# Attention loaded and computed by pairs of heads, the first batch's norm split into three steps, and leftover rows on a second DMA queue

## The chip, the cores and the metric

The kernel runs on one core of a Trainium2 chip. The metric is device time in microseconds (us); lower is better. The kernel before takes 851.52 us, the median of 9 runs (851.2 to 853.03).

Engines: PE (TensorE) multiplies matrices, DVE (VectorE) and ACT (ScalarE) work elementwise, SP (SyncE) issues DMAs. ACT can issue DMAs too. PE writes to PSUM banks, which DVE and ACT read.

## The reference, cut to what matters

```python
kv  = np.einsum('bhsd,bhse->bhde', k, v)        # 8 batches, 8 heads, 576 rows, 64 columns
out = np.einsum('bhsd,bhde->bhse', q, kv)
rms = np.sqrt(np.mean(out * out, axis=-1, keepdims=True) + 1e-06)
attn = out / rms * g_norm
x = attn.transpose(0, 2, 1, 3).reshape(8 * 576, 8 * 64)
a, b = x @ w1, x @ w2                           # 512 -> 1024
result = ((a * b) @ w3) @ w_out                 # 1024 -> 1024 -> 512
```

q, k, v and the result are fp32. The four weight matrices arrive as 64-bit floats and are converted on the chip.

## The kernel before, in words

The 576 rows of a batch are split into 512 rows (`G`), which are handled as a group of their own, and 64 leftover rows. The leftover rows of two batches make one tile of 128 rows, and those of all eight batches make a ninth group. The kernel computes `w3 @ w_out` once (the "fold") and then needs two products per group: the gates (`x @ w1`, `x @ w2`, multiplied) and the projection.

**The stages.** First comes the head: load batch 0, compute its attention. Then come the gates of group 0, made by plain matmuls in `gate` (L379), eight blocks `f` of 128 columns; block `f` needs its piece of w1 and w2, converted by `convert`. Then the fold: for each of eight blocks of w3, `turn_w3` (transposes, L406) and `fold_block` (L419), with the attention of batch 1 in pieces between them. Then project group 0, and a loop over groups `T` = 1 to 8: gates by a Strassen-Winograd scheme (`winograd`, L432) with the attention of batch `T + 1` in eight pieces between its products, then the projection, by `winograd` too.

**The attention of a batch** has these steps, and each works on half of the heads, four at a time:
- `load_half` (L91, L99): k, v and q of four heads, 512 KB each, and the leftover rows of k and v (`kl`, `vl`, 64 KB each). `load_left` (L105) loads the leftover rows of q (`ql`) for all heads.
- `kv` (L232): k transposed times v, 64 columns by 64, two heads above each other, five row blocks with the leftover rows as the last one. The result goes into the block-diagonal `kv_bd` by two DVE copies (L247) and two ACT copies (L245).
- `q_t` (L254): four transposes of q, then an ACT copy to `qT` (L256). It is called twice for each half.
- `product` (L295): q times kv, then `norm`: square on ACT (L272), sum on DVE (L274), square root on ACT (L280), reciprocal and multiply on DVE (L281, L282).
- `turn` (L327): four transposes, then ACT scales by `g_norm` into `xT` (L331).
- for odd batches `q_t_left` (L264), `product_left` (L312) and `turn_left` (L336) do the same for the leftover rows of two batches.

**Order.** PE's order is written out by hand over the whole kernel. In the head and the gates of group 0 the orders of DVE, ACT and SP are written out by hand as well; afterwards a scheduler orders these three. Every DMA goes out on SP's queue, in order. PSUM has five banks `mm` and three banks `at`; attention uses `at`. `keep_warm` (L215) issues matmuls whose result nobody reads.

In the head, batch 0 runs by halves: `kv0`, `q_t` twice, `product` twice, then the second half with the turns between. All of a product's norm is issued with it.

**Weights.** `load_raw` (L128) loads 1 MB of 64-bit words into one of four buffers; ACT (L142, L143) and DVE (L144, L147, L150, L154) convert it. `convert_next` converts the next block of a fixed list and then issues the load of the block four places on, which waits for that buffer. So SP's queue in the gate stage is a row of raw loads, with the loads of batch 1 between them; `load_left(1)` is the last thing that this stage issues, behind the raw loads.

**Pieces.** From batch 1 on, `attention(b)` returns eight lists of steps, and the fold or the gates call one list at each of eight places. In the fold a piece stands between `turn_w3` and `fold_block`. Before, the leftover rows have their places in the last three pieces:

```python
if b % 2:
    pieces[5] += [(q_t_left,)]
    pieces[6] += [(product_left,)]
    pieces[7] += [(turn_left,)]
```

Of the kernel before, what the change touches and what calls it, by code (L numbers as in the profile page):

```python
# [19 lines left out]
def kernel(  # L20
# [29 lines left out]
    nc = tc.nc  # L50
# [16 lines left out]
    inp = ctx.enter_context(tc.tile_pool(name="inp", bufs=1))  # L67
# [6 lines left out]
    early = tc.tile_pool(name="early", bufs=1)  # L74
# [6 lines left out]
    q_left = {}  # L81

    HB = H // 2

    def load_half(b, half, pool):

        heads = slice(half * HB, (half + 1) * HB)
        tiles = []
        for name, src in (("k", k), ("v", v), ("q", q)):
            t = pool.tile([P, HB, J * D], FP32, name=f"{name}_sb")  # L90
            nc.sync.dma_start(  # L91
                out=t, in_=src[b, heads, 0:G, :].rearrange("h (p j) d -> p h (j d)", j=J)
            )
            tiles.append(t)
            if name == "q":
                continue
            left = pool.tile([L, HB, D], FP32, name=f"{name}l_sb")
            tiles.append(left)
            nc.sync.dma_start(out=left, in_=src[b, heads, G:S, :].rearrange("h p d -> p h d"))  # L99
        loaded[b, half] = tiles  # L100

    def load_left(b):
        if b % 2 == 0:
            q_left[b // 2] = inp.tile([P, H, D], FP32, name="ql_sb")
        nc.sync.dma_start(  # L105
            out=q_left[b // 2][(b % 2) * L:(b % 2 + 1) * L],
            in_=q[b, :, G:S, :].rearrange("h p d -> p h d"),
        )
# [25 lines left out]
    def convert(dst, raw):  # L134
        if raw.dtype == FP32:
            nc.vector.tensor_copy(out=dst, in_=raw)
            return
        words = raw.bitcast(U32).rearrange("p (n w) -> p n w", w=2)
        lo, hi = words[:, :, 0], words[:, :, 1]
        low = conv_pool.tile([P, 1024], FP32, name="low", bufs=2)  # L140
        dst_bits, low_bits = dst.bitcast(U32), low.bitcast(U32)
        nc.scalar.activation(low, lo, AF.Copy, scale=2.0 ** -51, bias=2.0)  # L142
        nc.scalar.activation(dst, hi.bitcast(FP32), AF.Abs)  # L143
        nc.vector.tensor_scalar(  # L144
            out=dst, in0=dst, scalar1=LEAST, scalar2=MOST, op0=ALU.max, op1=ALU.min
        )
        nc.vector.tensor_scalar(  # L147
            out=dst_bits, in0=dst_bits, scalar1=3, scalar2=None, op0=ALU.logical_shift_left
        )
        nc.vector.scalar_tensor_tensor(  # L150
            out=low_bits, in0=hi, scalar=0x80000000, in1=low_bits,
            op0=ALU.bitwise_and, op1=ALU.bitwise_or,
        )
        nc.vector.tensor_tensor(out=dst_bits, in0=dst_bits, in1=low_bits, op=ALU.add)  # L154
# [27 lines left out]
    def convert_next(what):  # L182
# [9 lines left out]
        convert(dst, raws[n])  # L192
        converted.append(n)
        load_next()

# [5 lines left out]
    nc.scalar.activation(const.tile([P, 1], FP32, name="warm"), eps_col, AF.Sqrt)  # L201
# [16 lines left out]
    def attention(b):  # L218
# [4 lines left out]
        def kv(half):  # L223
            k_sb, kl_sb, v_sb, vl_sb, _ = loaded[b, half]
            n = HB // 2
            kv_ps = bank(ps_at, "at")[:, 0:n * D].rearrange("p (r e) -> p r e", r=n)
            for r in range(n):
                for j in range(J + 1):
                    cols = slice(j * D, (j + 1) * D)
                    for e in range(2):  # L230
                        h = 2 * r + e
                        nc.tensor.matmul(  # L232
                            kv_ps[e * D:(e + 1) * D, r, :],
                            lhsT=k_sb[:, h, cols] if j < J else kl_sb[:, h, :],
                            rhs=v_sb[:, h, cols] if j < J else vl_sb[:, h, :],
                            start=(j == 0),
                            stop=(j == J),
                        )
            for i in range(2):
                rows = slice(i * D, (i + 1) * D)  # L240
                to = bd[rows, half * HB:(half + 1) * HB, rows]
                to = to.rearrange("p (r e) d -> p r e d", e=2)
                for e in range(2):
                    if i:
                        nc.scalar.copy(to[:, :, e, :], kv_ps[e * D:(e + 1) * D])  # L245
                    else:
                        nc.vector.tensor_copy(out=to[:, :, e, :], in_=kv_ps[e * D:(e + 1) * D])  # L247

        def q_t(i, half):

            q_sb = loaded[b, half][-1]
            qt_ps = bank(ps_at, "at").rearrange("p (h t) -> p h t", h=HB)
            for h in range(HB):
                nc.tensor.transpose(qt_ps[:, h, :], q_sb[:, h, i * P:(i + 1) * P], ident)  # L254
            qT[i, half] = work.tile([P, HB, P], FP32, name="qT", bufs=4)
            nc.scalar.copy(qT[i, half], qt_ps)  # L256
# [10 lines left out]
        def norm(o_ps, dst):  # L267
# [11 lines left out]
            )  # L279
            nc.scalar.activation(inv, inv, AF.Sqrt, scale=1.0 / D, bias=eps_col)  # L280
            nc.vector.reciprocal(inv, inv)  # L281
# [9 lines left out]
        def product(i, half):  # L291

            o_ps = bank(ps_at, "at")
            for h in range(HB):
                nc.tensor.matmul(  # L295
                    o_ps[:, h * P:(h + 1) * P],
                    lhsT=qT[i, half][:, h, :],
                    rhs=bd[:, half * HB + h, :],
                    start=True,
                    stop=True,  # L300
                )
            st[i, half] = work.tile([P, 2, HB, D], FP32, name="xn", bufs=3)
            norm(o_ps, st[i, half].rearrange("p j h d -> p h j d"))

        def product_left():
            xn = st["left"] = work.tile([P, H, D], FP32, name="xn", bufs=3)
            for e in range(2):
# [11 lines left out]
                norm(o_ps, xn.rearrange("p (r e) d -> p r e d", e=2)[:, :, e:e + 1, :])  # L319

        def turn(i, half):

            n = HB // 2
            t_ps = bank(ps_at, "at").rearrange("p (r j t) -> p r j t", r=n, j=2)
            for j in range(2):
                for r in range(n):
                    nc.tensor.transpose(  # L327
                        t_ps[:, r, j, :], st[i, half][:, j, 2 * r:2 * r + 2, :], ident
                    )
            dst = x[:, half, i].rearrange("p r (j t) -> p r j t", j=2)  # L330
            nc.scalar.activation(dst, t_ps, AF.Copy, scale=g_col)  # L331
# [10 lines left out]

        if b == 0:

            return {name: lambda f=f, a=a: f(*a) for name, f, a in (
                (f"{f.__name__}{''.join(map(str, a))}", f, a)
                for f, *a in [(kv, 0), (kv, 1)] + [
                    (f, i, half) for f in (q_t, product, turn) for i in range(2) for half in range(2)
                ]
            )}  # L350

        pieces = []
        for half in range(2):
            pieces += [
                [(kv, half), (q_t, 0, half)],
                [(product, 0, half), (q_t, 1, half)],
                [(product, 1, half), (turn, 0, half)],
                [(turn, 1, half)],
            ]
        if b % 2:  # L360
            pieces[5] += [(q_t_left,)]
            pieces[6] += [(product_left,)]
            pieces[7] += [(turn_left,)]
# [230 lines left out]
    with tc.manual_schedule(  # L594
# [3 lines left out]
        load_half(0, 0, inp)  # L598
        load_half(0, 1, early_pool)
        g_src = g_norm.rearrange("(d o) -> d o", o=1)  # L600
        for e in range(2):
            nc.sync.dma_start(out=g_col[e * D:(e + 1) * D, :], in_=g_src)
        for _ in range(RAW):
            load_next()
        load_left(0)
        first = attention(0)
        keep_warm(16)
        for name in ("kv0", "q_t00", "q_t10", "product00", "product10"):
            first[name]()
        keep_warm(4)  # L610
        for name in ("kv1", "q_t01", "q_t11", "turn00", "product01", "turn10", "product11"):
            first[name]()
        keep_warm(4)
        for name in ("turn01", "turn11"):
            first[name]()
# [3 lines left out]
        for _ in range(2):  # L619
            convert_next("w")  # L620
        for f in range(KF):
            convert_next("w" if f + 2 < KF else "w3")
            if f % 2:
                convert_next("w_out")
            gate(0, f)
            if f == 3:
                load_half(1, 0, inp)
        load_left(1)
# [4 lines left out]
    for n, i in enumerate(FOLD_ORDER):  # L633
        if n + 2 < KF:
            convert_next("w3")
# [3 lines left out]
        if n == 1:  # L639
            load_half(1, 1, inp)  # L640
        fold_block(i)
    load_half(2, 0, inp)
    load_left(2)
# [11 lines left out]
    for T in range(1, NG):  # L655
        pieces = iter(attention(T + 1) if T + 1 < B else [])

        def between(n=[0]):
            n[0] += 1
            next(pieces, lambda: None)()  # L660
            if T + 1 < B and n[0] == 2:
                load_half(T + 1, 1, inp)
# [4 lines left out]
        if T + 2 < B:  # L667
            load_half(T + 2, 0, inp)
            load_left(T + 2)
# [33 lines left out]
```

## Time and profile before

| what | before |
|---|---|
| median of 9 runs (lowest, highest) | 851.52 us (851.2, 853.03) |
| the profiled execution's own time | 851.31 us |
| span of the profiled execution | 849.2 us |
| mean granted clock of TensorE | 0.993 of full speed |
| PE weight loads busy | 683.4 us (80%) |
| DMA traffic | 59.41 MB, mean 70 GB/s |

The profile shows one execution. The span is the time from its first to its last instruction; the execution's own time is 2.1 us longer. A line such as `L432` is a line of the kernel; `out<-in` names the tiles. Idle time of an engine that does not set the end costs nothing.

By stage, from the chain of work that ended last: head to 32.5 us, gates of group 0 to 89.3, fold to 165, and from there the projection of group 0 and the loop over the groups, to 849.2.

### The profile page before, as it was taken

How to read it: one execution, taken by the hardware profiler on the slowest of the kernel's cores; microseconds unless marked ns; L12 is line 12 of the kernel's file. 1: busy time of each engine (PE TensorE's matmuls, PEld its weight loads, DVE VectorE, ACT ScalarE, POOL GpSimd, SP SyncE). 2: the span in 40 equal slices, each digit the busy share in tenths (PEclk: the TensorE clock that was granted, in tenths of full speed). 3: DMA queues.
4: the chain of work that ended last, by engine and by line, in shares of the span. 5: the costliest groups of instructions: out<-in, count | busy, mean ns of one | idle time of the engine just before them, and what ended most of it. 6: DMA issues, size and time to landing. Idle time of an engine off the chain costs nothing.

```text
span 849.2 us, 10819 instructions
## 1 busy us (share of the span) xinstructions
PE 830.6 (98%) x4480; PEld 683.4 (80%) x4480; DVE 378.4 (45%) x718; ACT 249.1 (29%) x447; POOL 0.7 (0%) x6
## 2 busy tenths in 40 slices
PE   8599999999999999999999999999999999999997
PEld 7244556588888888888888888888888888888886
DVE  3798963493450455035504550355045503333430
ACT  3645532113321333133213331332133312212220
POOL 0000000000000000000000000000000000000000
PEclk9799999999999999999999999999999999999999
DMA  9768803003201221031012210320120000001002
GB/s 271 228 220 321 280 6 93 1 32 99 57 25 49 81 63 32 34 96 57 25 50 81 63 31 37 94 57 25 50 81 1 2 39 12 1 0 50 1 1 49
DMA packets 52112, 59.41 MB, mean 70 GB/s; under 512 B 14688, under 2 KB 47456, under 8 KB 51040
## 3 DMA queue, kind: packets, MB, share of 16 engines
q1 hardware_dynamic: 52064, 58.73, 22.0%
q8 instruction: 35, 0.57, 0.3%
q14 instruction: 13, 0.11, 0.0%
HBM read 49.28 MB, written 9.44 MB: 69 GB/s over the span
## 4 chain that ended last, share of the span: by engine, by line
PE 96%; DVE 1%; ACT 1%; DMA 1%; issue 0%; SPq 0%; ACTq 0%; DVEq 0%
PE mm L432 71%; PE mm L379 7%; PE mm L419 6%; PE at L295 3%; PE at L232 3%; PE at L254 2%; PE at L327 2%; PE at L312 1%; PE mm L406 1%; DMA v_sb<-in_v_dram 1%; DVE inv L274 0%; DVE xn L282 0%; PE at L336 0%; PE at L264 0%; ACT sq L272 0%
## 5 line engine op out<-in xcount | busy, mean ns | idle before, releaser
L432 PE MATMUL mm<-xT,w_sb 128*128 128x256 f32 x672 | 154.2, 379 | 0.0
L432 PEld LDWEIGHTS mm<-xT,w_sb 128*128 128x128 f32 x672 | 127.7, 190 | 17.4
L432 PE MATMUL mm<-xc,ws 128*128 128x256 f32 x512 | 115.7, 379 | 0.0
L432 PEld LDWEIGHTS mm<-xc,ws 128*128 128x128 f32 x512 | 97.3, 190 | 13.2
L445 ACT COPY u<-mm 128x512 f32<-128x512 f32 x82 | 48.1, 586 | 193.9 <-PE mm L432 193.9
L432 PE MATMUL mm<-w3o_sb,ab 128*128 128x256 f32 x432 | 96.2, 379 | 0.0
L432 PEld LDWEIGHTS mm<-w3o_sb,ab 128*128 128x128 f32 x432 | 82.1, 190 | 11.6 <-issue 0.5
L445 ACT COPY p<-mm 128x512 f32<-128x512 f32 x82 | 48.1, 586 | 139.2 <-PE mm L432 139.2
L432 PE MATMUL mm<-os,as 128*128 128x256 f32 x288 | 63.6, 379 | 0.0
L379 PE MATMUL mm<-xT,w_sb 128*128 128x512 f32 x128 | 56.7, 606 | 6.6 <-DVE w_sb L154 6.6
L432 PEld LDWEIGHTS mm<-os,as 128*128 128x128 f32 x288 | 54.7, 190 | 7.4
L432 PE MATMUL mm<-xc,w_sb 128*128 128x256 f32 x256 | 60.5, 379 | 0.0
L419 PE MATMUL mm<-wo_sb,w3T 128*128 128x512 f32 x128 | 56.4, 593 | 0.0
L274 DVE TENSOR_REDUCE inv<-sq 128x8 f32<-128x512 f32 (+1 forms) x40 | 25.1, 628 | 69.5 <-ACT sq L272 69.5
L379 PEld LDWEIGHTS mm<-xT,w_sb 128*128 128x128 f32 x128 | 24.9, 195 | 38.1 <-issue 30.5
L545 DVE TENSOR_TENSOR c<-mm,u 128x512 f32<-128x512 f32 x32 | 22.0, 688 | 73.9 <-PE mm L432 73.9
L432 PE MATMUL mm<-xT,ws 128*128 128x256 f32 x224 | 53.3, 381 | 0.0
L247 DVE COPY kv_bd<-at 64x128 f32<-64x128 f32 x32 | 9.2, 287 | 95.9 <-PE at L232 95.6
L432 PEld LDWEIGHTS mm<-xc,w_sb 128*128 128x128 f32 x256 | 46.8, 190 | 5.4
L419 PEld LDWEIGHTS mm<-wo_sb,w3T 128*128 128x128 f32 x128 | 23.7, 190 | 26.9 <-issue 26.8
L578 DVE TENSOR_TENSOR o_sb<-mm,u 128x512 f32<-128x512 f32 x9 | 6.2, 692 | 86.4 <-issue 74.0
L432 PEld LDWEIGHTS mm<-xT,ws 128*128 128x128 f32 x224 | 40.7, 190 | 4.7
(87 smaller groups left out, 920.6 us busy)
## 6 DMA issues: line engine op xcount, KB each, us to landing
k_sb<-in_k_dram SPq DMA_DIRECT2D x16, 512.0 KB, 4.4
v_sb<-in_v_dram SPq DMA_DIRECT2D x16, 512.0 KB, 5.3
q_sb<-in_q_dram SPq DMA_DIRECT2D x16, 512.0 KB, 4.0
raw<-in_moe_w_dram SPq DMA_DIRECT2D x16, 512.0 KB, 7.0
raw<-in_moe_w_dram SPq DMA_DIRECT2D x8, 1024.0 KB, 6.2
out_dram<-o_sb SPq DMA_DIRECT2D x16, 512.0 KB, 2.6
raw<-in_moe_w_out_dram SPq DMA_DIRECT2D x4, 1024.0 KB, 5.0
kl_sb<-in_k_dram SPq DMA_DIRECT2D x16, 64.0 KB, 4.3
```

The costliest lines, as they stand in the source:

```text
L232: nc.tensor.matmul(kv_ps[e * D:(e + 1) * D, r, :], lhsT=k_sb[:, h, cols] if j < J else kl_sb[:, h, :], rhs=v_sb[:, h, cols] if j < J else ...
L247: nc.vector.tensor_copy(out=to[:, :, e, :], in_=kv_ps[e * D:(e + 1) * D])
L254: nc.tensor.transpose(qt_ps[:, h, :], q_sb[:, h, i * P:(i + 1) * P], ident)
L274: nc.vector.tensor_reduce(out=inv, in_=sq[:, cols].rearrange("p (h d) -> p h d", d=D), axis=AX.X, op=ALU.add,)
L295: nc.tensor.matmul(o_ps[:, h * P:(h + 1) * P], lhsT=qT[i, half][:, h, :], rhs=bd[:, half * HB + h, :], start=True, stop=True,)
L312: nc.tensor.matmul(o_ps[l * L:(l + 1) * L, r * D:(r + 1) * D], lhsT=st["qT"][rows, r, l * L:(l + 1) * L], rhs=kv_bd[l][rows, 2 * r + e, rows],
L327: nc.tensor.transpose(t_ps[:, r, j, :], st[i, half][:, j, 2 * r:2 * r + 2, :], ident)
L379: nc.tensor.matmul(g_ps, lhsT=w_sb[:, f, w, c, :], rhs=xT[T][:, c // 2, :, c % 2, :], start=(c == 0), stop=(c == NP - 1),)
L419: nc.tensor.matmul(f_ps, lhsT=t[:, j, :], rhs=wo_sb[:, j, :], start=(j == 0), stop=(j == KF - 1))
L432: nc.tensor.matmul(ps[:, u, :], lhsT=lhsT(a_name, u, c), rhs=rhs(b_name, c),  start=(u == 0 and c == 0 and to is None), stop=(c == chunks ...
L445: nc.scalar.copy(t, ps)
L545: nc.vector.tensor_add(c, one, two)
```

## The change: pairs, a split norm, a second queue

- `load_half` becomes `load_pair`: k, v and q of two heads, 256 KB each, in two sets of buffers. The leftover rows of k and v are loaded for all eight heads at once (`load_kv_left`, 128 KB each); for batch 0 from ACT's queue, as is `g_col`.
- `kv`, `q_t`, `product` and `turn` take a pair of heads. Each is called four times per batch. One `q_t` or `product` of a pair has the four transposes or matmuls that one call had before; a `kv` has half as many as before, and its copies are 64 columns wide instead of 128.
- `norm` becomes a generator with two `yield`s: after the sum, and after the square root. Batch 0 uses them to place the parts between the steps of the next pair. All other callers run it through.
- The first block of weights of batch 0's gates is converted in two halves of 512 columns, around the last multiply and turn.
- The pieces of batches 1 to 7 are laid out anew, and the loads are issued from within them. `q_t_left` moves from piece 5 to piece 0.
- The load of `ql` for an even batch is issued in the piece 7 of the batch ahead of it, that for an odd batch in piece 0 of the batch ahead. For batches 0 and 1 it stays where it was.

```diff
+    def load_pair(b, r, pool):
+        tiles = []
+        for name, src in (("k", k), ("v", v), ("q", q)):
+            t = pool.tile([P, 2, J * D], FP32, name=f"{name}_sb")
+            nc.sync.dma_start(out=t,
+                in_=src[b, 2 * r:2 * r + 2, 0:G, :].rearrange("h (p j) d -> p h (j d)", j=J))
...
+    def load_kv_left(b, queue=nc.sync):
...
+    def convert_next(what, pieces=1):
...
+        size = 1024 // pieces
+        for j in range(pieces):
+            cols = slice(j * size, (j + 1) * size)
+            convert(dst[:, cols], raws[n][:, cols])
+            yield
...
+        def begin(r):
+            kv(r)
+            q_t(r)
+            if b and r + 2 < NP:
+                load_pair(b, r + 2, inp)
+            elif b and b + 1 < B:
+                load_pair(b + 1, r + 2 - NP, inp)
+                if r + 1 == NP:
+                    load_kv_left(b + 1)
...
+        pieces = [
+            [(begin, 0)],
+            [(middle, 0), (begin, 1)],
+            [(turn, 0), (middle, 1)],
+            [(begin, 2), (turn, 1)],
+            [(middle, 2), (begin, 3)],
+            [(turn, 2), (middle, 3)],
+            [(turn, 3)],
+            [],
+        ]
         if b % 2:
-            pieces[5] += [(q_t_left,)]
-            pieces[6] += [(product_left,)]
-            pieces[7] += [(turn_left,)]
+            pieces[0].append((q_t_left,))
+            pieces[6].append((product_left,))
+            pieces[7].append((turn_left,))
+            if b + 1 < B:
+                pieces[7].append((load_q_left, b + 1))
+        elif b + 1 < B:
+            pieces[0].append((load_q_left, b + 1))
...
-        load_half(0, 0, inp)
-        load_half(0, 1, early_pool)
+        load_kv_left(0, nc.scalar)
+        for r in range(2):
+            load_pair(0, r, inp)
...
+            nc.scalar.dma_start(out=g_col[e * D:(e + 1) * D, :], in_=g_src)
+        nc.scalar.activation(const.tile([P, 1], FP32, name="warm"), eps_col, AF.Sqrt)
...
-        keep_warm(16)
-        for name in ("kv0", "q_t00", "q_t10", "product00", "product10"):
-            first[name]()
-        keep_warm(4)
...
+        keep_warm(14)
+        for r in range(NP):
+            kv(r)
+            q_t(r)
+            if r:
+                all_of(steps)
+            keep_warm(2)
+            steps = product(r)
+            next(steps)
+            if r:
+                turn(r - 1)
+            next(steps)
+        block_0 = convert_next("w", 2)
+        all_of(steps)
+        next(block_0)
+        keep_warm(4)
+        turn(NP - 1)
+        all_of(block_0)
...
             gate(0, f)
             if f == 3:
-                load_half(1, 0, inp)
-        load_left(1)
+                load_pair(1, 0, inp)
+                load_kv_left(1)
+            elif f == 5:
+                load_pair(1, 1, inp)
+        load_q_left(1)
```

## The prediction

> **What bounds it now.** The first view is the page's list of busy engines, and then the list of TensorE's waits:
>
> ```profile
> PE 830.6 (98%) x4480; PEld 683.4 (80%) x4480; DVE 378.4 (45%) x718; ACT 249.1 (29%) x447; POOL 0.7 (0%) x6
> ```
>
> ```profile
> PE mm L379 <- DVE w_sb L154: 6.6, 1, 6.6
> PE at L327 <- DVE xn L282: 1.4, 1, 1.4
> PE mm L215 <- POOL ident masks.py:199: 1.4, 1, 1.4
> PE at L295 <- ACT qT L256: 0.9, 1, 0.9
> ```
>
> PE is busy 98% and every wait of it happens once, before 32.52 us, where the first gate matmul (L379) starts. From there to the end PE never waits. So the change can win only ahead of 32.52, and behind it any added PE time, or any wait that reaches PE, counts in full. The stage view with the granted clock (columns: stretch, its length, PE busy (count), granted clock, DMA share, GB/s) shows what the 6.65 us wait costs besides:
>
> ```profile
> 25.90:32.50 6.60, 0.00 (x0) 0.50 0.30 65
> 32.50:36.00 3.50, 3.48 (x5) 0.55 0.80 287
> 36.00:40.00 4.00, 4.00 (x11) 1.00 0.80 272
> ```
>
> After the gap the first four records of gate matmuls (each fp32 matmul leaves two) follow each other at 0.85 us instead of 0.43: 1.7 us more.
>
> **1. The head, -5.0.** Durations are those of the timeline of before. The first kv needs k and v of two heads (256 KB each) and kl, vl of all eight (128 KB each), 0.77 MB; before, 1.09 MB had to land, from about 1.9 to 7.42 us, 0.2 MB/us. That gives 5.8 us if nothing else is in the way. But kl and vl have 256-byte packets and now share the DMA engines with the SP queue, so q and the second pair may come between: 1.28 MB, 8.3 us. The 14 warm-up matmuls end at 6.4 and hold PE anyway. I take 7.3 for vl, nearest to the row of v (7.42), and 7.75 for the first DVE copy into kv_bd (9.42 before).
>
> The Trainium skill ("DMA: Bandwidth & Descriptors", section "Issuing engines are not separate DMA queues") says that DMAs of several issuing engines run on the same 16 DMA engines and that a second issuer saves only issue time. By it the second queue is worth the two issues ahead of v and q (0.74 and 0.63 us), and the first copy would come at about 8.0, the total 0.3 us later than mine. The trace agrees as far as it goes: from 0.9 to 25.3 us the DMA share is 1.04.
>
> From that copy: two DVE copies 0.44 (half the columns of the 0.29 us copies, so an estimate), hop 0.09, two ACT copies 0.44, qT 0.63: first product at 9.35. From there each pair is one loop through three engines: product to square 1.20, square 0.63, reduce 0.61, the next pair's DVE copies 0.44, hop 0.09, ACT copies 0.44, qT 0.63 = 4.04 us. The split norm is what puts the next copies right behind the reduce; the square root, reciprocal and multiply lie beside the copies, and the turn lies in ACT's wait for the reduce. Last product 9.35 + 3 x 4.04 = 21.5; square 22.7, reduce 23.3, root 24.0; ACT's two half conversions end at 25.35; DVE's half needs 2.1 (half of 28.65 to 32.52, plus 0.1 for four starts). First gate at 27.5: 5.0 us earlier. The last turn (about 26.8) and the second half (DVE to 29.8, needed after four matmuls) are covered. Bounds: kv_bd copy at 7.3 or 8.5, and 0.15 per pair in the loop, so 3.5 to 6.
>
> The gap in front of the gate is now split (some 1.6 us, a turn, 1.5 us). The row 22.00 to 25.30 of the same view has 1.20 us busy in 3.30, and 0.50 was granted next; so I expect the slow start again, a little shorter: -0.3, bounds -1.7 and 0.
>
> DVE starts the second block 2.4 us after the gate instead of just ahead of it. Its waits at L390 (1.39 and 1.27 us in the first gates) take that up; PE finds block 1 ready 2.4 us early, so nothing. The halved conversion adds starts, counted above.
>
> **2. A wait moved into the fold, +6.3.** `q_t_left` of batch 1 moves from piece 5 to piece 0, right behind the first `kv` and `q_t`. Its rows ql come by a load which SP issues only after the weights queued ahead of it, and that place does not move. The timeline of SP and the DMA issues from 85 to 110 us (KB each, us to landing):
>
> ```profile
> 80.03 9.75 SPq L128 DMA_DIRECT2D raw<-in_moe_w_dram  x3
> 89.84 1.45 SPq L105 DMA_DIRECT2D ql_sb<-in_q_dram  x1
> ```
>
> ```profile
> ql_sb<-in_q_dram SPq DMA_DIRECT2D x1, 128.0 KB, 8.3
> ```
>
> The last of those raw loads waits for the conversion of the last w_out block (L150 at 88.17), and DVE there is paced by PE through L390. So the load keeps its place against the end of the gates however early these start. ql lands at 98.1 on the clock of before. When does PE ask for it?
>
> ```profile
> 90.94 0.69 PE L232 MATMUL at<-v_sb,k_sb 128*64 128x64 f32 x16
> 91.55 0.33 PE L232 MATMUL at<-vl_sb,kl_sb 64*64 64x64 f32 x4
> 91.81 0.69 PE L232 MATMUL at<-v_sb,k_sb 128*64 128x64 f32 x16
> ```
>
> One pair of kv takes 90.94 to 91.81, four q transposes 0.49 more: 92.3. Before, ql was read at 138.7 and nobody noticed. PE now waits 5.8 us; in the landing records 15 of its 16 parts were there at 95.7 and one came late, without which it is 3.4. I take 5.0. Behind that transpose on PE stands the whole fold (L419) and everything after; on ACT the copy of qT_left, with conversions behind it, and on DVE the copy of the first folded block. All shift by the same amount; the PE order then has no wait to give back. On SP the loads of ql for batches 2 and 3 wait for the same transposes, and pair 3 behind them; its use lies four pieces later (over 30 us), so nothing.
>
> After such a wait the clock is low again: up to the 1.7 us above, 0 if it holds; I take 1.3. The Trainium skill ("TensorE: Matmul & The Clock Gate", section "HAM oscillation — how this bites in real kernels") says that PE gaps over about 3.4 us halve the clock; the trace agrees with its 0.50 and 0.55. By it a 5 us wait costs the full 1.7, and the total would be 0.4 us higher.
>
> **3. Four groups of kv in a batch instead of two, +2.2.** The timeline of PE in the steady part:
>
> ```profile
> 192.46 1.89 PE L432 MATMUL mm<-xc,ws 128*128 128x256 f32 x8
> 194.28 0.69 PE L232 MATMUL at<-v_sb,k_sb 128*64 128x64 f32 x16
> 195.15 0.69 PE L232 MATMUL at<-v_sb,k_sb 128*64 128x64 f32 x16
> 196.03 0.66 PE L254 MATMUL at<-ident,q_sb 128*128 128x128 f32 x4
> 196.52 0.38 PE L432 MATMUL mm<-xT,ws 128*128 128x256 f32 x1
> ...
> 202.60 0.60 PE L254 MATMUL at<-ident,q_sb 128*128 128x128 f32 x4
> 203.03 0.38 PE L432 MATMUL mm<-xc,w_sb 128*128 128x256 f32 x1
> ```
>
> Eight records of gate matmuls at 0.216 end their turn at 194.18; kv starts at 194.28, 0.10 for the change of shape. A pair takes 0.875. Four q transposes take 0.49 behind kv and 0.43 behind a product. A half was 0.10 + 1.75 + 0.49 + 0.43 = 2.77; two pairs are 2 x (0.10 + 0.875 + 0.49) = 2.93. That is 0.16 per half, fourteen times in batches 1 to 7: 2.2 us, all on PE. Bounds 1.5 and 2.9. Products, turns and leftovers keep their counts. Smaller DVE and ACT copies (two and two per pair) run beside 5 to 7 us of gate matmuls per piece. Each pair's load is requested three pieces (some 24 us) ahead of its use; landings take about 5.
>
> **Sum.** -5.3 + 6.3 + 2.2 = +3.2 on the profiled execution (span 849.2, own time 851.31): 854.5. That run lies 0.2 under the median of nine, 851.52, so 854.7 is forecast.
>
> **Rivals.** *ql is there in time (faster).* If the load landed by 93.8, 4.0 us after its issue, term 2 would fall below 1.5 and the head would decide; without term 2 the sum is -3.1, 848.4. For it: ql's median is 4.9 us. Against it: its shortest landing in the trace is 4.3, and here a 1 MB raw load stands just ahead. 0.08.
>
> *A short wait.* No late DMA engine, 3.4 us, and 1.0 for the clock: -5.3 + 4.4 + 2.2 = +1.3, 852.8. The late part was one of 16 in one execution. 0.20.
>
> *The head gives less.* ACT issues four DMAs before its table load, and the second of g_col waits for kl's landing; if kl is late among the small packets, ACT's first copy is, and the head gains 3 while term 2 is 7.5: +6.7, 858.2. Against it: kl should land near 5.5, and table load and warm-up (1.5 us) then end before the copy at 8.3. 0.17.
>
> The forecast itself has 0.55, with 853.2 to 856.5 as its own range. A measurement of this kernel can tell 0.2%, 1.7 us, from no change: faster is under 849.8, slower over 853.2. The rival that is faster gives 0.08; the short wait most of the 0.20 for same; forecast and last rival 0.72 for slower. The range 850.8 to 858.5 leaves out the first rival and the far end of the last.
>
> **What would show it.** Of after: first gate matmul near 27.5; a PE wait of about 5 us on DMA ql_sb at the transposes of `q_t_left`, right behind the first kv after the gates, with the granted clock near 0.5 behind it; from there no wait; four kv groups per batch with 0.10 us in front of each; the last project as long as before. Wrong if no wait on ql_sb appears, or if the gates wait for DVE.

## The result, and the profile after

| what | before | after |
|---|---|---|
| median on the chip of this comparison (lowest, highest) | 851.90 us (851.20, 853.87) | 855.45 us (852.61, 856.69) |
| ratio of after to before, 95% interval | | 1.0037 [1.0029, 1.0045] |
| profiled execution: own time, span | 851.31, 849.2 us | 848.74, 846.9 us |
| mean granted clock in it | 0.993 | 0.999 |

After is slower by 3.55 us. The profiled execution of after is faster than every timed one, so its trace shows where the work lies, and what it lacks against the timed ones has to come from other executions. A second session with the same unaltered kernel gave 853.73 us against 852.26, 1.0025 [1.0012, 1.0037], and a trace of 853.20 us own time. Both traces are read here; the second is called "after, second trace".

The list of busy engines and the list of TensorE's waits, of after:

```profile
PE 831.2 (98%) x4484; PEld 683.1 (81%) x4484; DVE 379.8 (45%) x754; ACT 255.5 (30%) x481; POOL 0.7 (0%) x6
```

```profile
PE at L306 <- ACT qT L263: 2.7, 4, 1.1
PE at L271 <- DMA ql_sb<-in_q_dram: 2.6, 1, 2.6
PE mm L400 <- DVE w_sb L155: 1.7, 1, 1.7
PE at L336 <- DVE xn L291: 1.5, 1, 1.5
```

The 6.6 us wait ahead of the gates is gone: waits of 1.5 and 1.7 us are left, on the two sides of the last turn. A new wait on `ql_sb` has come, at the line of `q_t_left` (L271). In the second trace it is longer:

```profile
PE at L271 <- DMA ql_sb<-in_q_dram: 3.8, 1, 3.8
```

TensorE's timeline of after shows the place (start, duration, line, operation, in brackets the idle time ahead); the matmuls of the fold come next:

```profile
86.14 0.66 PE L261 MATMUL at<-ident,q_sb 128*128 128x128 f32 x4
89.37 0.66 PE L271 MATMUL at<-ident,ql_sb 128*128 128x128 f32 x4 [2.57 <-DMA ql_sb<-in_q_dram]
89.87 7.03 PE L440 MATMUL mm<-wo_sb,w3T 128*128 128x512 f32 x16
```

and SyncE's timeline the load that it waits for, behind three raw weight loads whose issue was held up:

```profile
74.36 9.74 SPq L129 DMA_DIRECT2D raw<-in_moe_w_dram  x3
...
84.15 1.17 SPq L106 DMA_DIRECT2D ql_sb<-in_q_dram  x1
```

PE asks at 86.63 (the end of four transposes, 86.14 + 0.49), 2.5 us after the issue; the data came 5.2 us after it.

By stages, read from the starts of PE's records, the traces of before and after compare as follows. All values are in us. "Gates" runs from the first gate to the first transposes of w3; "fold" and "rest" each run from the start of their first matmul to the start of their last, and "rest" begins with the first projection.

| trace | first gate | gates | gates to first fold matmul | fold | rest | span |
|---|---|---|---|---|---|---|
| before | 32.52 | 56.58 | 4.09 | 71.22 | 678.18 | 849.2 |
| after | 28.39 | 55.04 | 6.44 | 71.58 | 678.86 | 846.9 |
| after, second trace | 28.32 | 56.70 | 7.62 | 73.27 | 678.86 | 851.4 |

The head gave 4.1 to 4.2 us. The wait took 2.4 to 3.5 of it back, and the rest 0.7. The two traces of after differ by 4.5 us in span; 1.7 of that is in the gates and 1.7 in the fold, the two stages that follow a gap, and 1.2 is the wait. The windows with the granted clock say why. Columns: stretch, length, PE busy (count), granted clock, DMA share, GB/s. First after, then the second trace:

```profile
28.40:32.00 3.60, 3.60 (x9) 1.00 0.24 31
91.00:95.00 4.00, 4.00 (x10) 1.00 0.99 327
```

```profile
28.40:32.00 3.60, 3.60 (x5) 0.54 0.21 36
91.00:95.00 4.00, 2.86 (x8) 0.77 1.01 369
```

In the same stretch one execution got through nine records of gate matmuls and the other through five. So the low clock behind a gap is granted in some executions and not in others, and the first profile is one that was spared twice.

### The profile page after: what moved, and what is told of

The parts are those of the page before. It is cut to its first block, busy times and chain, and to the rows that moved or that the text cites. A ratio compares the mean times of both kernels' runs of the same rounds, so it can differ in the third digit from the quotient of the medians.

```text
span 846.9 us, 10941 instructions
## 1 busy us (share of the span) xinstructions
PE 831.2 (98%) x4484; PEld 683.1 (81%) x4484; DVE 379.8 (45%) x754; ACT 255.5 (30%) x481; POOL 0.7 (0%) x6
## 4 chain that ended last, share of the span: by engine, by line
PE 96%; DVE 2%; ACT 1%; DMA 1%; issue 0%; POOLq 0%; SPq 0%; POOL 0%; ACTq 0%; DVEq 0%
PE mm L453 71%; PE mm L440 7%; PE mm L400 6%; PE at L306 4%; PE at L239 3%; PE at L261 2%; PE at L336 1%; PE at L323 1%; PE mm L223 1%; PE mm L427 1%; DMA ql_sb<-in_q_dram 1%; DVE low L151 0%; DVE inv L281 0%; ACT sq L279 0%; ACT qT L263 0%
## 5 line engine op out<-in xcount | busy, mean ns | idle before, releaser
L400 PE MATMUL mm<-xT,w_sb 128*128 128x512 f32 x128 | 55.2, 593 | 1.7 <-DVE w_sb L155 1.7
L400 PEld LDWEIGHTS mm<-xT,w_sb 128*128 128x128 f32 x128 | 24.2, 190 | 32.0 <-issue 29.9
L567 DVE TENSOR_TENSOR ab<-c 128x256 f32<-128x256 f32 x96 | 40.7, 424 | 2.8
```

Of the source, the lines that this page charges most:

```text
L400: nc.tensor.matmul(g_ps, lhsT=w_sb[:, f, w, c, :], rhs=xT[T][:, c // 2, :, c % 2, :], start=(c == 0), stop=(c == NP - 1),)
L567: nc.vector.tensor_mul(dst, c[:, 0, :], c[:, 1, :])
```

## The experiments

The first four runs test the prediction's account as a whole: an earlier head, against a wait on ql with a lower clock behind it. The later ones take its parts one by one. Each expectation names the theories that it sets against each other. Every kernel was compared with before on its own chip. "Stage" values are read as in the table above.

### The same kernel again

No edit.

> The changed kernel once more, unaltered, for a second profile. Its first profile (848.74 us, granted clock 0.999) is faster than all its timed runs (852.6 to 856.7, clocks 0.991 to 0.997). Theory A: the timed runs pay a half clock after the two gaps of PE (ahead of the first gate, and at the wait on ql_sb), and a longer wait; then a typical profile has a time of 853 to 857, a wait on ql_sb of 3 to 6 us, and granted clocks near 0.5 behind one or both gaps; the steady part (from the first projection on) is as long as in the first profile, 679 us. Theory B: the time is lost somewhere in the steady part, by waits that the first profile did not have; then that part is 4 to 8 us longer.

Measured: 853.73 us (851.87 to 856.93, 12 runs), 1.0025 [1.0012, 1.0037]. The wait on ql was 3.8 us, the low clock followed both gaps, and the rest was 678.86 in both traces, to the hundredth. So what differs between these two traces lies ahead of the first projection, and not in the steady part.

Every execution also has its mean granted clock on record. In the 22 timed executions of the two sessions the time goes with it: at 0.996 or more they took 851.87 to 853.63 us, at 0.992 or less 855.69 to 856.93. Of the ten in the first session one is of the first kind and five of the second; of the twelve in the second, five and four.

### Is it the wait? Three ways to move it

`left_late`: after, with the transposes of ql back in the piece where before had them (the rest stays 678.85). `load_early`: the transposes stay, but the load goes out behind the gates of block 3. `before_left0`: the kernel before, with only this move made.

```diff
left_late
-            pieces[0].append((q_t_left,))
+            pieces[5].append((q_t_left,))
load_early
                 load_kv_left(1)
+                load_q_left(1)
             elif f == 5:
                 load_pair(1, 1, inp)
-        load_q_left(1)
before_left0
-            pieces[5] += [(q_t_left,)]
+            pieces[0] += [(q_t_left,)]
```

> The changed kernel with q_t_left moved back from piece 0 to piece 5. Theory A (the wait on ql_sb and the half clock behind it cost 4 to 7 us): no wait on ql_sb, 849 to 851 us, some 5 us under the changed kernel. Theory B (the loss is elsewhere): no more than 1 us under it, 854 to 856.

> The changed kernel with q_t_left left in piece 0, and the load of batch 1's ql issued earlier, next to the loads of kl and vl at gate block 3. Theory A (the wait is for the load's place in SP's queue): no wait on ql_sb, the same time as with q_t_left in piece 5, 849 to 851. Theory C (piece 0 itself is the wrong place, by what is queued behind it on ACT or by PSUM banks): time stays at 854 to 856, with a wait on something else.

> The kernel before with nothing but q_t_left moved from piece 5 to piece 0. Theory A: a wait on ql_sb of 3.4 to 4.9 us (the first half's kv takes 0.9 us longer than a pair's, so PE asks later) and up to 1.7 us of half clock: 855.5 to 858.5 us against 851.9. Theory B: no change beyond 1 us.

Measured, beside 853.73 for after and 852.26 for before: `left_late` 848.19 (848.17 to 850.26), 0.9964 [0.9952, 0.9976]; `load_early` 848.62 (846.39 to 849.38), 0.9957 [0.9944, 0.9969]; `before_left0` 857.53 (854.63 to 858.22), 1.0060 [1.0048, 1.0073]. The first two came out 0.4 to 0.8 us under the 849 to 851 that was foretold. Neither has a wait on ql_sb in its list (`left_late` has 0.5 us on a conversion there instead). The third has, and its windows show the gap and what follows it:

```profile
PE at L264 <- DMA ql_sb<-in_q_dram: 4.5, 1, 4.5
```

```profile
92.90:97.40 4.50, 0.68 (x8) 1.00 1.02 344
97.40:101.00 3.60, 2.91 (x7) 0.56 0.86 271
```

Taking the wait out of after is worth 5.5 us by the place and 5.1 by the load; putting it into before costs 5.3. The three agree. Without the wait what is left of the change is a gain of 4.1 us over before (852.26 - 848.19). The wait turned the sign.

How long the wait is depends on the landing, which varies by execution. Thirteen traces issue this load of 128 KB behind the same raw loads. It landed after 5.2 us in after's first trace, 6.4 in its second, 8.0 in `before_left0` and 8.3 in before; the median of the thirteen is 6.4. In the landing records 15 of the load's 16 parts are there after 5.2 to 6.2 us in every trace; what varies is the last part, which comes 1.4 to 2.4 us behind the others in six of them and at most 0.7 behind in the rest. The eight traces that have the changed kernel's loads lie between 5.2 and 7.8. PE asks 2.5 us after the issue in after; so, as an estimate from these landings, the wait can be from 2.7 to 5.3 us.

### What the gaps ahead of the gates cost in clock

Dummy matmuls into the gaps: in `left_late_warm` on both sides of the last turn, in `before_warm` into the 6.6 us.

```diff
left_late_warm (on left_late)
-        keep_warm(4)
+        keep_warm(10)
         turn(NP - 1)
+        keep_warm(8)
before_warm
+            if f == 0:
+                keep_warm(22)
             gate(0, f)
```

> The changed kernel with q_t_left in piece 5 and the two gaps of PE ahead of the first gate filled with warm-up matmuls (10 instead of 4 ahead of the last turn, 8 more behind it; they end before the gate can start). Theory A (the half clock behind the gap costs up to 1.7 us, and its phase is what spreads the times): the gate stage is 55.0 us instead of 56.7, time 846.5 to 847, little spread. Theory B (no clock effect, or the added matmuls get in the way): 848.2 as with q_t_left in piece 5 alone, or up to 0.5 more.

> The kernel before with 22 warm-up matmuls in its 6.6 us gap ahead of the first gate. Theory A: the first gate starts at 32.5 as before, the gate stage falls from 56.6 to 55.0 us, time 850.2 to 850.6. Theory B: no change, 851.9. It prices the half clock alone, without anything of the change.

Measured: `left_late_warm` 846.87 us (846.74 to 847.21), 0.9939 [0.9927, 0.9951]; `before_warm` 849.93 (849.62 to 850.15), 0.9973 [0.9964, 0.9983], each against 852.15. The gate stage is 55.04 us in both, the value of after's first trace, and the spread shrinks from some 2 us to 0.5. `left_late_warm` has the full clock where its gates begin:

```profile
28.43:32.00 3.57, 3.57 (x10) 1.00 0.22 34
```

In `before_warm`, whose time lies a little under the 850.2 to 850.6 foretold, that prices the low clock at 1.5 us in the trace (56.58 to 55.04) and 2.2 in the median. Three other traces with before's head had 56.87 to 57.09 us of gates, so the price of the low clock is not fixed: `load_early`'s trace shows 0.50 from its first gate at 28.37 up to 33.80 and has the longest gate stage, 57.72.

The Trainium skill ("TensorE: Matmul & The Clock Gate", section "HAM oscillation — how this bites in real kernels") has PE gaps over about 3.4 us lower the clock. At the wait on ql the traces agree: 2.6 us kept 1.00, 3.8 was followed by 0.77 and 4.5 by 0.56. Ahead of the gates no single gap of the change is that long: the two waits are 1.5 and 1.65 us, with the turn between them. Together they are a stretch of 3.8 us with 0.66 us of transposes in it. Behind it after's first trace kept 1.00, its second got 0.54. So such a stretch can cost the clock as well, in some executions; whether the short gaps add up, or the transposes between them count for little, no run here tells apart.

### The groups of kv

`kv_together` keeps pairs, but puts two `kv` side by side again (and the leftover transposes back in piece 5). `before_kv_split` is the kernel before with each half's `kv` cut in two groups, a `q_t` behind each.

```diff
kv_together
...
-            [(begin, 0)],
-            [(middle, 0), (begin, 1)],
-            [(turn, 0), (middle, 1)],
-            [(begin, 2), (turn, 1)],
-            [(middle, 2), (begin, 3)],
-            [(turn, 2), (middle, 3)],
-            [(turn, 3)],
-            [],
+            [(kv, 0), (kv, 1), (q_t, 0), (load, 2)],
+            [(middle, 0), (q_t, 1), (load, 3)],
+            [(middle, 1), (turn, 0)],
+            [(turn, 1)],
+            [(kv, 2), (kv, 3), (q_t, 2), (load, 4)],
+            [(middle, 2), (q_t, 3), (load, 5)],
+            [(turn, 2), (middle, 3)],
+            [(turn, 3)],
...
-            pieces[0].append((q_t_left,))
-            pieces[6].append((product_left,))
+            pieces[5].append((q_t_left,))
+            pieces[6].insert(1, (product_left,))
before_kv_split
...
-                [(kv, half), (q_t, 0, half)],
-                [(product, 0, half), (q_t, 1, half)],
+                [(kv, half, [0]), (q_t, 0, half), (kv, half, [1]), (q_t, 1, half)],
+                [(product, 0, half)],
```

> The changed kernel with the pieces of batches 1 to 7 laid out so that the kv of two pairs stand next to each other again (two groups in a batch), q_t_left in piece 5, product_left ahead of the last product. Theory A (each extra group of kv costs 0.15 us of PE): the part from the first projection on is 1.8 us shorter than the changed kernel's 678.9, and the time 2 us under that with q_t_left in piece 5 alone: 846 to 846.5. Theory B (the order of the groups costs nothing on PE, or a wait for a PSUM bank takes its place): 848 to 849.

> The kernel before, where in batches 1 to 7 the kv of a half is split in two groups of one pair each, with the q transposes of the first behind the first group and those of the second behind the second. Theory A: 14 more groups at 0.15 us: the part from the first projection on rises from 678.2 to 680.0, time 853.8 to 854.2. Theory B: nothing, 851.9.

Measured, against 852.15 for before: `kv_together` 845.41 us (843.63 to 847.07), 0.9920 [0.9907, 0.9933]; its rest is 677.05, 1.81 less than the 678.86 of after. `before_kv_split` 853.50 (853.02 to 854.35), 1.0018 [1.0009, 1.0026]; its rest is 679.99, 1.81 more than the 678.18 of before. The rest holds the attention of batches 2 to 7, so twelve extra groups: 0.15 us each, in both directions. The other moves in `kv_together` do not enter: the place of the leftover transposes left the rest at 678.85 in `left_late`, and the leftover product takes 1.47 us in `kv_together` as in after. Both medians lie 0.3 to 0.6 us under the ranges foretold. TensorE's timeline shows the group, first in after, then in `kv_together`:

```profile
191.32 0.69 PE L239 MATMUL at<-v_sb,k_sb 128*64 128x64 f32 x16
191.93 0.33 PE L239 MATMUL at<-vl_sb,kl_sb 64*64 64x64 f32 x4
192.19 0.66 PE L261 MATMUL at<-ident,q_sb 128*128 128x128 f32 x4
```

```profile
189.08 0.69 PE L239 MATMUL at<-v_sb,k_sb 128*64 128x64 f32 x16
189.70 0.33 PE L239 MATMUL at<-vl_sb,kl_sb 64*64 64x64 f32 x4
189.96 0.66 PE L261 MATMUL at<-ident,q_sb 128*128 128x128 f32 x4
```

A pair takes the same 0.87 us in both; so what a group of its own adds lies at its edges.

### Two good parts together

`kv_together_warm` has the edits of `kv_together` and of `left_late_warm`.

> All mends together: the changed kernel's head, kv of two pairs next to each other, q_t_left in piece 5, product_left ahead of the last product, both gaps filled with warm-up matmuls. If the terms add up: gate stage 55.0 us, the part from the first projection on 677.05, median 843.5 to 844.2 with little spread. Rival: the warm matmuls only help where the clock had fallen, so its fastest run is no better than the 843.6 of the kernel without them.

Measured: 844.21 us (843.93 to 845.11, 4 runs), 0.9910 [0.9896, 0.9923], against 851.90. This is the upper end of the 843.5 to 844.2 that the sum of the terms had given. It beats before by 7.7 us, but its lowest time is no better than the 843.63 of `kv_together`: the dummy matmuls take away the upper part of the spread and no more.

### The two parts of the head

Both on `left_late`. `one_queue` puts the leftover rows of k and v and `g_col` of batch 0 back on SyncE's queue. `norm_whole` issues a product's norm in one go.

```diff
one_queue
-        load_kv_left(0, nc.scalar)
-        for r in range(2):
-            load_pair(0, r, inp)
+        load_pair(0, 0, inp)
+        load_kv_left(0)
+        load_pair(0, 1, inp)
...
-            nc.scalar.dma_start(out=g_col[e * D:(e + 1) * D, :], in_=g_src)
+            nc.sync.dma_start(out=g_col[e * D:(e + 1) * D, :], in_=g_src)
norm_whole
-            if r:
-                all_of(steps)
             keep_warm(2)
             steps = product(r)
-            next(steps)
+            all_of(steps)
             if r:
                 turn(r - 1)
-            next(steps)
```

> The changed kernel with q_t_left in piece 5 and the leftover rows of k and v and g_norm of batch 0 back on SP's queue (after the first pair). Theory A (the DMA engines are shared, a second queue saves issue time only): first gate within 0.5 us of 28.1 to 28.4, time 847.7 to 848.7. Theory B (the second queue brings the first kv forward by over 1 us): gate at 29.3 or later, 849.5 or more.

> The changed kernel with q_t_left in piece 5 and batch 0's norm run through at once behind each product, not in three steps. Theory A (the split puts the next pair's kv copies right behind the sum; without it DVE holds them behind root, reciprocal and multiply, some 1.3 us per pair, three times): first gate 3 to 4 us later, at 31.5 to 32, time 851.5 to 852.5. Theory B (the copies wait for PE anyway): no change, 848.2.

Measured, against 851.90 for before: `one_queue` 847.51 us (847.00 to 848.67), 0.9951 [0.9938, 0.9963], beside 0.9964 [0.9952, 0.9976] for `left_late`. The intervals overlap: the second queue gives nothing that can be measured in the time. By the Trainium skill ("DMA: Bandwidth & Descriptors", section "Issuing engines are not separate DMA queues") a second issuer saves issue time only; the runs agree, with the DMA share of 1.04 that the prediction read in before's head, and even that saving does not show in the time. In its one trace the first copy into `kv_bd` comes at 8.61 and the first gate at 28.86, within what theory A allowed; eight traces with two queues have 7.88 to 8.73 for that copy, so a saving of half a microsecond is neither shown nor ruled out. The first copy into `kv_bd`, which the prediction put at about 8.0 by this rule and at 7.75 by its own estimate, came at 8.12 in after:

```profile
8.12 0.48 DVE L253 COPY kv_bd<-at 64x64 f32<-64x64 f32 x2 [5.08 <-PE at L239]
```

`norm_whole` 853.83 (852.86 to 854.63, 11 runs), 1.0022 [1.0014, 1.0031]. Its first gate is at 33.00 instead of 28.14, and gate and time both lie above what was foretold (31.5 to 32, 851.5 to 852.5). DVE's timeline of after comes first, then DVE's and PE's of `norm_whole`:

```profile
12.26 0.47 DVE L253 COPY kv_bd<-at 64x64 f32<-64x64 f32 x2
12.66 0.19 DVE L290 RECIPROCAL inv<-inv 128x8 f32<-128x8 f32 x1
12.88 0.69 DVE L291 TENSOR_TENSOR xn<-at,inv 128x512 f32<-128x512 f32 x1
```

```profile
13.05 0.69 DVE L291 TENSOR_TENSOR xn<-at,inv 128x512 f32<-128x512 f32 x1
13.66 0.46 DVE L253 COPY kv_bd<-at 64x64 f32<-64x64 f32 x2
```

```profile
15.24 1.16 PE L306 MATMUL at<-kv_bd,qT 128*128 128x128 f32 x8 [2.30 <-ACT qT L263]
...
18.77 0.66 PE L261 MATMUL at<-ident,q_sb 128*128 128x128 f32 x4 [1.06 <-ACT xT L338]
...
20.68 1.16 PE L306 MATMUL at<-kv_bd,qT 128*128 128x128 f32 x8 [0.80 <-ACT qT L263]
```

The copies into `kv_bd` come behind the multiply, at 13.66, where after has them ahead of the reciprocal and the multiply, at 12.26. In addition the next q transposes wait for the turn's copy, which the expectation had not counted. The loop is 5.4 us per pair instead of 4.1. So the head's gain needs the split norm: with pairs and a second queue but without the split, the first gate comes no earlier than before's 32.52. Whether the split would give it alone, by halves, was not run.

### Where does the leftover product get cheaper?

PE's timelines of before and of after show the leftover product (`product_left`) and the matmuls behind it:

```profile
324.82 1.92 PE L312 MATMUL at<-kv_bd,qT_left 64*64 64x64 f32 x32
326.67 0.70 PE L432 MATMUL mm<-xT,ws 128*128 128x256 f32 x2
```

```profile
322.91 1.54 PE L323 MATMUL at<-kv_bd,qT_left 64*64 64x64 f32 x32
324.37 0.92 PE L453 MATMUL mm<-xT,ws 128*128 128x256 f32 x3
```

Up to the next instruction it takes 1.85 us in before and 1.46 to 1.47 in after, in all four odd batches. To see whether its place does it, `before_left_first` puts it ahead of the other steps of its piece.

```diff
-            pieces[6] += [(product_left,)]
+            pieces[6].insert(0, (product_left,))
```

> The kernel before with product_left ahead of the product and the turn in piece 6 of odd batches, not behind them. In the changed kernel the 32 matmul records of product_left take 1.47 us instead of 1.85 with equal operands. Theory A (its place behind the product makes its second half start anew, 0.2 us, and its first half's rows not overlap with the second's): 0.38 us less in each of four batches, the part from the first projection on 677.0 instead of 678.2, time 850.4. Theory B (it comes from loads or buffers of the change): 851.9.

Measured: 853.25 us (852.43 to 853.81, 11 runs) against 851.90, 1.0012 [1.0003, 1.0021]; a gain was expected (850.4), and this is a miss. PE's timeline of it:

```profile
324.81 1.54 PE L312 MATMUL at<-kv_bd,qT_left 64*64 64x64 f32 x32
326.28 1.16 PE L295 MATMUL at<-kv_bd,qT 128*128 128x128 f32 x8
327.92 0.63 PE L327 MATMUL at<-ident,xn 128*128 128x128 f32 x4 [0.49 <-DVE xn L282]
```

The leftover product did fall to 1.47, but the turn behind it now starts 1.64 us after the product's start, where before's started 0.89 after it. The rest is 679.07, 0.89 more than before's. DVE's timeline names the wait: its multiply `xn` for the first half of the leftover product starts at 327.35 and takes 0.42, and the turn starts at 327.92. The code explains it: attention has three PSUM banks `at`; the leftover product takes two, the product the third, and the turn needs a fourth.

The same count reads before. There the order is product, turn, leftover product, so the second half of the last one needs a fourth bank. ACT's copy of the turn, which frees one, runs from 325.05 for 0.68 us, to 325.73. PE's windows of before, for the leftover product alone, thin out just then:

```profile
325.40:325.60 0.20, 0.20 (x9) 1.00 0.00 0
325.60:325.80 0.20, 0.20 (x5) 1.00 0.00 0
325.80:326.00 0.20, 0.20 (x3) 1.00 0.00 0
326.00:326.20 0.20, 0.20 (x9) 1.00 0.00 0
```

The middle of the same group in after, where turn and leftover product are three banks in all:

```profile
323.50:323.70 0.20, 0.20 (x12) 1.00 0.00 0
323.70:323.90 0.20, 0.20 (x12) 1.00 0.00 0
323.90:324.10 0.20, 0.20 (x10) 1.00 0.00 0
```

This hold of 0.38 us stands in no list of waits, since the trace shows PE busy all through. That the banks are its cause is read from these times and the code in three kernels; a kernel with a fourth bank was not run, so the cause is argued and not shown.

## Why the prediction was right, and where its steps were off

The sign, the mechanism and the place were right: an earlier head, outweighed by a wait on ql that the moved transposes brought to PE. The forecast of 854.7 lies 0.8 us under the first session's 855.45 and 1.0 above the second's 853.73. That it comes so near is in part luck, as the terms show. Of the named signs, the gates began 0.9 later than the 27.5 foretold, the wait stood where it was said to, and no later wait came: PE's 1.7 us on DVE at L400 is the foretold one ahead of the first gate. The rival "the head gives less" did not come: ACT's table load was over at 6.64, and its first copy at 8.63 waited for DVE and not for the table. By terms:

**The head, -5.0: measured -4.1 to -4.4.** The first copy into `kv_bd` came at 8.12 instead of 7.75, the loop was 4.12 us instead of 4.04 (products at 9.72, 13.85, 17.97 and 22.08), and from the last product to the gate it was 6.3 instead of 6.0. In the other traces of before's head the first gate stood at 32.24 to 33.19, so one pair of traces gives this term to some half a microsecond. The reason given for the loop, copies right behind the reduce, is shown by `norm_whole`, which loses 4.9. The second queue, which the term counted as 0.3 us, is worth nothing that could be measured.

**The clock behind that gap, -0.3.** Where it is granted low the gates take 56.6 to 57.7 us, where not 55.04. Against before's 56.58 the two traces of after differ by -1.5 and +0.1, so a fixed value was the wrong form for this term. Its bounds, -1.7 and 0, hold the first of these and miss the second by 0.1; `load_early`'s 57.72 is 1.1 above. `before_warm` puts what before loses there at 2.2 in the median.

**The wait, +6.3: 5.1 to 5.5 by the second session's medians.** The wait itself was 2.6 and 3.8 in the two traces of after and 4.5 in `before_left0`, where 5.0 was taken. PE did ask 2.5 us after the issue, as worked out; the landing took 5.2 and 6.4 us instead of the 8.3 of before's trace, which is the latest of thirteen. The late part, which the prediction knew from that one execution, came in six of the thirteen. The half clock behind the wait was 1.7 (fold 73.27 against 71.58) or none. The rival "a short wait" (3.4 and 1.0) describes the two traces; by these medians the term lies between its 4.4 and the 6.3 of the forecast.

**The extra groups, +2.2: this step failed.** The price of a group was right: 0.15 us, fourteen times 2.1. What was wrong is "Products, turns and leftovers keep their counts", taken to mean that they keep their time. The leftover product fell by 0.38 in each of four odd batches, 1.5 in all, so that by this sum the steady part costs 0.6 and not 2.2, below the bound of 1.5; in the rest, with twelve groups and three odd batches, 1.81 - 1.14 = 0.67, and 0.68 was measured.

**The sum.** The head fell 0.6 to 0.9 short of its term, the wait was 0.8 to 1.2 too dear and the steady term 1.6, so the errors cancelled only in part. With the measured sizes it comes to -4.2 + 5.3 + 0.6 = +1.7, half of the +3.2 that was forecast and near the second session's difference (1.5). The first session's 3.55 is 2 us larger. Its only trace had no low clock behind the gaps and an early landing, so it can't say where those 2 us lay. The granted clock on record was low in more of that session's executions; but in the three traces with a wait on ql the longer wait also has the lower clock behind it, so whether the load or the clock came first stays open, and that the first session's time falls so near the forecast is luck. That trace alone, 848.74 us, would have told of a faster kernel.

## What to carry to other kernels

When a step that reads a load is moved earlier, compare its new time with the issue of that load and not with the step's old slack; if the step moves, move the load too, or leave it: either repair here turned a loss into a gain of about 4 us. Look at the landing of that load in several executions, since one may be early or late. Count PSUM banks along the new order as well as matmuls: a group can be held without a wait in the trace, here 0.38 us that the bank count explains. And fill short gaps ahead of long matmul stages where the granted clock behind them varies: here it took 1.2 to 2.2 us off the median and narrowed the spread.

## What the runs showed that had not been expected

- Two gaps of 1.5 and 1.65 us with 0.66 us of transposes between them were followed by a granted clock of 0.54 in one execution and 1.00 in another of the same kernel; the gates took 56.70 and 55.04 us.
- One profiled execution can lie outside all timed ones: 848.74 us against 852.61 to 856.69.
- The leftover product's 32 matmul records take 1.47 us in after and 1.85 in before, where by the code their second half meets no free bank, with PE shown as busy in both.
- The load of `ql` for batch 1, 128 KB behind the same raw loads, landed 5.2 us after its issue in one trace and 8.3 us in another; 15 of its 16 parts are there after 5.2 to 6.2 us, and the last one makes the difference.
